# W_out products four steps behind W_in products instead of three, with a smaller space for GpSimd's DMA descriptors

## The chip, the core and the metric

The kernel runs on one core of a Trainium2 chip. The metric is device time in microseconds (us) of one execution; the time of a kernel is the median of its runs. The core has a matrix engine (TensorE, PE in the profile, with its weight loads as PEld), VectorE (DVE), ScalarE (ACT), GpSimd (POOL) and SyncE (SP), each with a queue of its own that is worked in order, and 16 DMA engines. Results of TensorE go to banks of PSUM, from which VectorE and ScalarE read.

## The reference

```python
def _attn_ref(x, w_r, w_i, b_r, b_i):          # x: 8 x 3008 x 256
    X = np.fft.rfft(x, axis=1)
    Xr, Xi = X.real.astype(np.float32), X.imag.astype(np.float32)
    Yr = Xr @ w_r - Xi @ w_i + b_r             # w_r, w_i: 256 x 256
    Yi = Xr @ w_i + Xi @ w_r + b_i
    Yr = np.sign(Yr) * np.maximum(np.abs(Yr) - 0.01, 0.0)
    Yi = np.sign(Yi) * np.maximum(np.abs(Yi) - 0.01, 0.0)
    y = np.fft.irfft(Yr.astype(np.float64) + 1j * Yi.astype(np.float64), n=x.shape[1], axis=1)
    return y.astype(np.float32)

def _moe_ref(x, w_in, w_out):                  # x: 24064 x 256, w_in: 256 x 2048
    h = x @ w_in
    g = h * np.cos(h)
    return (g @ w_out).astype(np.float32)      # w_out: 2048 x 256
```

The output of the first function, seen as 24064 tokens of 256 values, is the input of the second.

## The kernel before, in words

**Two halves that run interleaved.** For each of the 8 batches a Fourier half computes y (transforms as small matmuls, the products with w_r and w_i, the threshold, and the way back), and a second half, called MoE here, computes (h·cos h) @ w_out from it. While the MoE half of batch b runs, the Fourier work of batch b+1 is pulled in between its steps. `ahead` makes that work as a sequence of pieces with a planner's costs, and `pull` takes pieces as long as a budget, topped up at each step, allows it.

**MoE tiling.** Each batch has 6 token tiles (t) of 512 tokens (448 in the last), and each tile 16 chunks (f) of 128 hidden features. One (b, t, f) is a step; there are 768, and I number them through: step 16 is the first of tile t=1, step 96 the first of batch b=1, so step 227 is f=3 of t=2 in b=2.

**One step.** `moe_step` issues the W_in product of a step: every operand is split into a high part of TensorE's fp32r format and a rest, so it takes 6 matmuls into one PSUM bank `ph` (L923, L924, L925). From `ph` a chain of five instructions leads to g: ScalarE forms the integer k (L932), VectorE subtracts it (r, L933), ScalarE takes the sine (L935), VectorE multiplies by h (the product, L936, which sets `ph` free), and ScalarE casts to the high part `gh` (L938). The rest gl = u − gh follows on GpSimd for f%4 of 0 and 2 (L325) and on VectorE otherwise (L328). `u`, `gh` and `gl` are tiles in SBUF with a number of buffers each.

**W_out behind W_in.** The W_out product of a step, `second`, is not issued with its W_in product but SKEW steps later; a list `pend` holds the steps between. It takes 6 matmuls into two PSUM tiles `po` (L905, L906 with gh, L909 with gl), which add up over the 16 steps of a token tile. After the last one ScalarE copies both `po` to an SBUF tile `ob` (L913) and SyncE stores them. There is one buffer for each of the two `po` tiles, so the first W_out of a token tile waits for the copies of the tile before it.

**The Fourier work beside it** shares all engines: among it casts on ScalarE to `Xh` (L594, L602, L609), rests `Xl` on VectorE (through L328 as well), transposes on VectorE (L716, L717), matmuls such as L660 that use Xh and Xl, and loads of `xt` that GpSimd issues and then uses (L450). All matmul results except po go through a ring of 6 PSUM banks.

**What sets the order.** The code sets a program order, and the framework's scheduler puts each engine's instructions into the order that they have on the chip. A change in SKEW so moves instructions on every engine, not on PE alone.

Of the kernel before, what the change touches and what calls it, by code (L numbers as in the profile page):

```python
# [13 lines left out]
F32 = mybir.dt.float32  # L14
# [13 lines left out]
F64_HUGE = float(np.uint32((1150 << 20) | 0xFFE00).view(np.float32))  # L28
NFC = FF // 128
NTT = 6  # L30
SKEW = 3
XP_BUFS = 6
W_AT = (8, 16, 24, 32, 40, 48, 56, 64, 74)
W_ORDER = tuple(range(16))
# [142 lines left out]
def tile_body(ctx: ExitStack, tc, x, w_r, w_i, b_r, b_i, w_in, w_out,  # L177
              c_fq, c_sig, c_f3, c_ff, c_if, c_iw, c_sgn, out):
    nc = tc.nc
# [6 lines left out]
    pool = {}  # L186
# [145 lines left out]
    def fps(name):  # L332
        if len(ring) >= BANKS:
            assert ring[-BANKS][1]
        p = ps.tile([128, 512], F32, tag="f", name=name, bufs=BANKS)
        if "pro" not in pool:
            ring.append((p, []))
        return p
# [3 lines left out]
    def drained(p, ins):  # L342

        for q, readers in (side if "pro" in pool else ring)[-BANKS:]:
            if q is p:
                readers.append(ins.ins)
# [551 lines left out]
    def second(b, t, f, gh, gl):  # L898
        n = 512 if t < NTT - 1 else 448
        if f == 0:  # L900
            outs[0] = [ps.tile([128, 512], F32, tag=f"o{e}", name=f"po{e}", bufs=1) for e in range(2)]
        po = outs[0]
        for e in range(2):
            es = slice(128 * e, 128 * e + 128)
            mm(po[e][:, :n], wo[0][:, 0, f, es], gh[:, :n], start=f == 0, stop=False)  # L905
            mm(po[e][:, :n], wo[0][:, 1, f, es], gh[:, :n], start=False, stop=False)  # L906
        for e in range(2):
            es = slice(128 * e, 128 * e + 128)
            mm(po[e][:, :n], wo[0][:, 0, f, es], gl[:, :n], start=False, stop=f == NFC - 1)  # L909
        if f == NFC - 1:  # L910
            ob = stage_out("ob")
            for e in range(2):
                nc.scalar.copy(ob[:, 512 * e:512 * e + n], po[e][:, :n])  # L913
                nc.sync.dma_start(out[b, e, :, 512 * t:512 * t + n], ob[:, 512 * e:512 * e + n])

    def moe_step(b, t, f, pull):
        th, tl = xT[b, t]
        n = 512 if t < NTT - 1 else 448
        ph = fps("ph")
        h = ph[:, :n]  # L920
        fs = slice(128 * f, 128 * f + 128)
        for c in range(2):
            mm(h, win[:, 0, c, fs], th[:, c, :n], start=c == 0, stop=False)  # L923
            mm(h, win[:, 0, c, fs], tl[:, c, :n], start=False, stop=False)  # L924
            ins = mm(h, win[:, 1, c, fs], th[:, c, :n], start=False, stop=c == 1)  # L925
        if (b, t) == (0, 0) and f < 4:
            mark["ph"] = ins
        u = pool["mo"].tile([128, 512], F32, tag="u", name="u", bufs=4)
        k = u.bitcast(I32)
        gh = pool["mo"].tile([128, 512], F32R, tag="gh", name="gh", bufs=SKEW + 1)  # L930
        gl = pool["mo"].tile([128, 512], F32R, tag="gl", name="gl", bufs=SKEW + 1)
        nc.scalar.activation(k[:, :n], h, AF.Identity, bias=0.25, scale=1.0 / TWO_PI)  # L932
        nc.vector.scalar_tensor_tensor(out=u[:, :n], in0=h, scalar=1.0 / TWO_PI, in1=k[:, :n],  # L933
                                       op0=ALU.mult, op1=ALU.subtract)
        nc.scalar.activation(u[:, :n], u[:, :n], AF.Sin, bias=HALF_PI, scale=TWO_PI)  # L935
        product = nc.vector.tensor_tensor(out=u[:, :n], in0=h, in1=u[:, :n], op=ALU.mult)  # L936
        drained(ph, product)
        step = [nc.scalar.copy(gh[:, :n], u[:, :n])]  # L938
        step.append((rest_pool if f % 4 in POOL_GL else rest)(gl[:, :n], u[:, :n], gh[:, :n]))
        if f % 4 in POOL_GL:  # L940
            step.append(product)
        elif steps:
            step.append(steps[-1][1])
        steps.append(step)
        pend.append((b, t, f, gh, gl))
        pull()
        if len(pend) > SKEW:
            second(*pend.pop(0))
        pull()
# [93 lines left out]
    for b in range(NB):  # L1043
        fa = ahead(b)
        for t in range(NTT):
            budget = [0.0]
            open_ = [True]
            rate = (C_COST + share(b)) / (NFC - 1) / 2

            def pull():  # L1050
                budget[0] += rate
                while open_[0] and budget[0] > 0:
                    c = next(fa, None)
                    if c is None:
                        open_[0] = False
                    else:
                        budget[0] -= c

            for f in range(NFC):
                if (b, t) == (0, 0) and f in W_LATE:  # L1060
                    next(mw, None)
                moe_step(b, t, f, pull)
            while open_[0]:
                c = next(fa, None)
                if c is None:
                    open_[0] = False
            del xT[b, t]
# [27 lines left out]
```

## Time and profile before

| | |
|---|---|
| Runs | 2622.96, 2630.61 and 2635.15 us, median 2630.61 |
| Profiled execution | 2636.05 us, of which the span of the trace is 2634.3 |
| Granted clock of PE, mean | 0.992 |
| Busy share of the span | PE 98%, PEld 79%, VectorE 74%, ScalarE 62%, GpSimd 37% |
| Chain of work that ended last | PE 81%, VectorE 9%, ScalarE 3%, DMA 2% |

The busy share says how much of the span an engine worked; PE's matmuls overlap one another, so its share comes out a little high. The chain is followed back from the last instruction to whatever released each one. It lies mainly on PE; where it leaves PE, PE was waiting. The granted clock is the share of full speed that PE's clock was allowed in a stretch; full speed is 2.4 GHz, and the other level is 1.2 GHz.

### The profile page before, as it was taken

What the parts mean: (1) busy time and instruction counts of PE and PEld (TensorE: products, weight loads), DVE (VectorE), ACT (ScalarE), POOL (GpSimd) and SP (SyncE); (2) the same over time, 40 slices, a digit from 0 to 9 for tenths busy, and PEclk for the clock granted to TensorE, in tenths of its full rate; (3) what the DMA queues carried; (4) which work ended last, traced back from release to release, by engine and by line L of the source; (5) the groups of instructions that cost most, each with busy time, mean ns of one, the idle gap of its engine ahead of it and who ended that gap; (6) DMA issues with size and microseconds to landing.
All of it is one profiled execution on the core that took longest, in us unless ns stands there. A gap on an engine that the chain in (4) does not pass through costs nothing.

```text
span 2634.3 us, 42943 instructions
## 1 busy us (share of the span) xinstructions
PE 2571.2 (98%) x15961; PEld 2072.1 (79%) x15961; DVE 1943.9 (74%) x3089; ACT 1630.0 (62%) x3003; POOL 976.7 (37%) x946
## 2 busy tenths in 40 slices
PE   9899899999999999999999999999999999999999
PEld 7478678877788777887778877888778888888888
DVE  5688667877768777687776877778776777766665
ACT  5565556665666556656566565665666666666665
POOL 1124443444424443244433445334432333422222
PEclk9999999999999999999999999999999999999999
DMA  6534435354434443334442544326432343210000
GB/s 209 179 102 130 137 109 147 87 146 131 119 86 112 140 128 102 95 108 129 128 117 79 138 133 135 89 87 164 129 100 89 93 111 116 69 38 31 17 25 16
DMA packets 172953, 283.11 MB, mean 107 GB/s; under 512 B 15608, under 2 KB 114200, under 8 KB 169160
## 3 DMA queue, kind: packets, MB, share of 16 engines
q1 hardware_dynamic: 161896, 243.78, 32.9%
q0 software_dynamic: 10112, 35.53, 4.3%
q8 instruction: 126, 2.06, 0.3%
q10 hardware_dynamic: 736, 1.05, 0.1%
q14 instruction: 83, 0.68, 0.1%
HBM read 149.76 MB, written 130.55 MB: 106 GB/s over the span
## 4 chain that ended last, share of the span: by engine, by line
PE 81%; DVE 9%; ACT 3%; DMA 2%; issue 2%; POOL 1%; SPq 0%; DVEq 0%; ACTq 0%; POOLq 0%
PE ph L923 12%; PE po L905 11%; PE ph L924 11%; PE ph L925 11%; PE po L906 11%; PE po L909 11%; PE pw L660 2%; PE pw L661 2%; PE pw L662 2%; DVE u L936 2%; DVE u L933 2%; PE pc L377 1%; PE pb L377 1%; DVE Xl L328 1%; PE pw L656 1%
## 5 line engine op out<-in xcount | busy, mean ns | idle before, releaser
L325 POOL TENSOR_TENSOR gl<-u,gh 128x512 fp32r<-128x512 f32 (+1 forms) x384 | 501.4, 1306 | 1135.4 <-ACT gh L938 942.8
L935 ACT ACTIVATE u<-u 128x512 f32<-128x512 f32 (+1 forms) x768 | 478.1, 623 | 392.7 <-DVE u L933 391.8
L933 DVE SCALAR_TENSOR_TENSOR u<-ph,u 128x512 f32<-128x512 f32 (+1 forms) x768 | 513.6, 671 | 248.3 <-ACT u L932 247.2
L936 DVE TENSOR_TENSOR u<-ph,u 128x512 f32<-128x512 f32 (+1 forms) x768 | 518.0, 675 | 236.6 <-ACT u L935 225.4
L905 PE MATMUL po<-gh,wout 128*128 128x512 f32 (+1 forms) x1536 | 602.4, 392 | 28.0 <-ACT gh L938 28.0
L938 ACT CAST gh<-u 128x512 fp32r<-128x512 f32 (+1 forms) x768 | 467.8, 609 | 257.7 <-DVE u L936 254.6
L923 PE MATMUL ph<-xTh,win 128*128 128x512 f32 (+1 forms) x1536 | 605.2, 394 | 9.3 <-DVE u L936 7.6
L932 ACT ACTIVATE u<-ph 128x512 int32<-128x512 f32 (+1 forms) x768 | 447.7, 586 | 262.4 <-PE ph L925 255.9
L924 PE MATMUL ph<-xTl,win 128*128 128x512 f32 (+1 forms) x1536 | 597.2, 389 | 0.1
L925 PE MATMUL ph<-xTh,win 128*128 128x512 f32 (+1 forms) x1536 | 596.6, 388 | 0.0
L906 PE MATMUL po<-gh,wout 128*128 128x512 f32 (+1 forms) x1536 | 595.5, 388 | 0.0
L909 PE MATMUL po<-gl,wout 128*128 128x512 f32 (+1 forms) x1536 | 476.3, 388 | 0.3 <-POOL gl L325 0.2
L923 PEld LDWEIGHTS ph<-xTh,win 128*128 128x128 f32 x1536 | 290.0, 189 | 101.0 <-DVE u L936 22.5
L905 PEld LDWEIGHTS po<-gh,wout 128*128 128x128 f32 x1536 | 289.4, 188 | 100.6 <-ACT gh L938 38.5
L328 DVE TENSOR_TENSOR gl<-u,gh 128x512 fp32r<-128x512 f32 (+1 forms) x384 | 297.8, 776 | 79.6 <-ACT gh L938 73.5
L925 PEld LDWEIGHTS ph<-xTh,win 128*128 128x128 f32 x1536 | 290.2, 189 | 57.3
L909 PEld LDWEIGHTS po<-gl,wout 128*128 128x128 f32 x1536 | 287.2, 188 | 60.8 <-issue 4.9
L924 PEld LDWEIGHTS ph<-xTl,win 128*128 128x128 f32 x1536 | 290.3, 189 | 51.1 <-DVE xTl L891 0.6
L906 PEld LDWEIGHTS po<-gh,wout 128*128 128x128 f32 x1536 | 289.7, 189 | 50.9
L709 POOL TENSOR_TENSOR odd<-st 128x184 f32<-128x184 f32 (+1 forms) x112 | 67.4, 604 | 147.2 <-DVE st L686 117.0
L328 DVE TENSOR_TENSOR Xl<-z,Xh 128x384 fp32r<-128x384 f32 x112 | 110.3, 1013 | 12.0 <-ACT Xh L594 8.9
L660 PE MATMUL pw<-Xh,wf 128*128 128x384 f32 x336 | 115.5, 344 | 2.4 <-ACT Xh L609 2.2
(123 smaller groups left out, 2453.1 us busy)
## 6 DMA issues: line engine op xcount, KB each, us to landing
scrF<-at SPq DMA_DIRECT2D x28, 1024.0 KB
z<-scrF SPq DMA_DIRECT2D x112, 256.0 KB
scrT<-tr SPq DMA_DIRECT2D x56, 512.0 KB
y<-scrT SPq DMA_DIRECT2D x112, 256.0 KB
bt<-scr SPq DMA_DIRECT2D x94, 256.0 KB
scr<-ao SPq DMA_DIRECT2D x84, 256.0 KB
scr<-bo SPq DMA_DIRECT2D x224, 96.0 KB
out_dram<-ob SPq DMA_DIRECT2D x80, 256.0 KB
```

What stands on the lines that cost most here:

```text
L325: return nc.gpsimd.tensor_tensor(out=lo, in0=x, in1=hi.bitcast(F32), op=ALU.subtract)
L905: mm(po[e][:, :n], wo[0][:, 0, f, es], gh[:, :n], start=f == 0, stop=False)
L906: mm(po[e][:, :n], wo[0][:, 1, f, es], gh[:, :n], start=False, stop=False)
L909: mm(po[e][:, :n], wo[0][:, 0, f, es], gl[:, :n], start=False, stop=f == NFC - 1)
L923: mm(h, win[:, 0, c, fs], th[:, c, :n], start=c == 0, stop=False)
L924: mm(h, win[:, 0, c, fs], tl[:, c, :n], start=False, stop=False)
L925: ins = mm(h, win[:, 1, c, fs], th[:, c, :n], start=False, stop=c == 1)
L932: nc.scalar.activation(k[:, :n], h, AF.Identity, bias=0.25, scale=1.0 / TWO_PI)
L933: nc.vector.scalar_tensor_tensor(out=u[:, :n], in0=h, scalar=1.0 / TWO_PI, in1=k[:, :n], op0=ALU.mult, op1=ALU.subtract)
L935: nc.scalar.activation(u[:, :n], u[:, :n], AF.Sin, bias=HALF_PI, scale=TWO_PI)
L936: product = nc.vector.tensor_tensor(out=u[:, :n], in0=h, in1=u[:, :n], op=ALU.mult)
L938: step = [nc.scalar.copy(gh[:, :n], u[:, :n])]
```

## The change

SKEW becomes 4, so that a W_out product follows its W_in product by four steps. `gh` and `gl` have SKEW + 1 buffers and so get a fifth; `u` gets one too, by number. Each of the three is 2 KB in every partition. The room comes from the space that is set aside in SBUF for the descriptors of GpSimd's DMAs, 16384 bytes in each partition without the new argument and 8192 with it. The instructions and their number stay the same.

```diff
-SKEW = 3
+SKEW = 4
...
-        u = pool["mo"].tile([128, 512], F32, tag="u", name="u", bufs=4)
+        u = pool["mo"].tile([128, 512], F32, tag="u", name="u", bufs=5)
         k = u.bitcast(I32)
         gh = pool["mo"].tile([128, 512], F32R, tag="gh", name="gh", bufs=SKEW + 1)
         gl = pool["mo"].tile([128, 512], F32R, tag="gl", name="gl", bufs=SKEW + 1)
...
-    nc = _bacc.Bacc("TRN2", target_bir_lowering=False, num_devices=1)
+    nc = _bacc.Bacc("TRN2", target_bir_lowering=False, num_devices=1,
+                     dynamic_dma_scratch_size=8192)
```

How the order moves, at the places of which the prediction speaks.

ScalarE around the change from tile t=1 to t=2 in batch 2, from k(226) on, before. `u<-ph` is k, `u<-u` the sine, `gh<-u` the cast of a step; the two `ob<-po` are the copies that set the PSUM tiles of the old token tile free:

```order
L932 ACTIVATE u<-ph 128x512
L913 COPY ob<-po_8384 128x512
L913 COPY ob<-po_8385 128x512
L935 ACTIVATE u<-u 128x512
L932 ACTIVATE u<-ph 128x512
L938 CAST gh<-u 128x512
L594 CAST Xh<-z 128x2x8x24
L602 CAST Xh<-z 128x2x8x24 x2
L932 ACTIVATE u<-ph 128x512
```

The same place now:

```order
L932 ACTIVATE u<-ph 128x512
L935 ACTIVATE u<-u 128x512
L932 ACTIVATE u<-ph 128x512
L938 CAST gh<-u 128x512
L594 CAST Xh<-z 128x2x8x24
L602 CAST Xh<-z 128x2x8x24 x2
L913 COPY ob<-po_8421 128x512
L913 COPY ob<-po_8422 128x512
L935 ACTIVATE u<-u 128x512
```

The two copies stood right behind k(226) and now stand behind gh(226) and three casts of the Fourier work.

ScalarE around the change from t=2 to t=3 in batch 1, before; the first row is k(146), the first `gh<-u` is that of 146:

```order
L932 ACTIVATE u<-ph 128x512
L935 ACTIVATE u<-u 128x512
L913 COPY ob<-po_5754 128x512
L913 COPY ob<-po_5755 128x512
L938 CAST gh<-u 128x512
L594 CAST Xh<-z 128x2x8x24 x2
L932 ACTIVATE u<-ph 128x512 x2
```

The same place now:

```order
L932 ACTIVATE u<-ph 128x512
L935 ACTIVATE u<-u 128x512
L938 CAST gh<-u 128x512
L594 CAST Xh<-z 128x2x8x24
L932 ACTIVATE u<-ph 128x512
L594 CAST Xh<-z 128x2x8x24
L935 ACTIVATE u<-u 128x512
L932 ACTIVATE u<-ph 128x512
L913 COPY ob<-po_5775 128x512
L913 COPY ob<-po_5776 128x512
```

The copies stood ahead of gh(146) and now stand behind it, two casts, k(147), the sine of 147 and k(148).

## Rows read from the trace of the kernel before

**Rows 1.** Page, part 1: busy time, share of the span, instructions of each engine

```profile
PE 2571.2 (98%) x15961; PEld 2072.1 (79%) x15961; DVE 1943.9 (74%) x3089; ACT 1630.0 (62%) x3003; POOL 976.7 (37%) x946
```

**Rows 2.** Page, part 5, groups: busy us, mean ns | idle before, releaser

```profile
L933 DVE SCALAR_TENSOR_TENSOR u<-ph,u 128x512 f32<-128x512 f32 (+1 forms) x768 | 513.6, 671 | 248.3 <-ACT u L932 247.2
L938 ACT CAST gh<-u 128x512 fp32r<-128x512 f32 (+1 forms) x768 | 467.8, 609 | 257.7 <-DVE u L936 254.6
L932 ACT ACTIVATE u<-ph 128x512 int32<-128x512 f32 (+1 forms) x768 | 447.7, 586 | 262.4 <-PE ph L925 255.9
```

**Rows 3.** Waits, PE and PEld: us in total, times, longest us

```profile
PE po L905 <- ACT gh L938: 28.0, 15, 5.1
PE pc L367 <- DMA bt<-scr: 3.3, 1, 3.3
PEld po L905 <- ACT gh L938: 38.5, 25, 5.5
```

**Rows 4.** Timeline of PE, step f=3 of t=2: start, us, instruction [idle, releaser]

```profile
599.21 0.50 PE L905 MATMUL po<-gh,wout 128*128 128x512 f32 x1 [0.51 <-ACT gh L938]
...
917.45 0.50 PE L905 MATMUL po<-gh,wout 128*128 128x512 f32 x1 [1.85 <-ACT gh L938]
...
1235.37 0.52 PE L905 MATMUL po<-gh,wout 128*128 128x512 f32 x1 [2.10 <-ACT gh L938]
...
1553.66 0.50 PE L905 MATMUL po<-gh,wout 128*128 128x512 f32 x1 [0.63 <-ACT gh L938]
...
1871.03 0.50 PE L905 MATMUL po<-gh,wout 128*128 128x512 f32 x1 [1.85 <-ACT gh L938]
```

**Rows 5.** Timeline ahead of step 227 (b=2, t=2, f=3), 911 to 915 us

```profile
911.09 0.66 DVE L936 TENSOR_TENSOR u<-ph,u 128x512 f32<-128x512 f32 x1
...
911.36 0.39 PE L905 MATMUL po<-gh,wout 128*128 128x512 f32 x1
...
911.78 0.62 ACT L938 CAST gh<-u 128x512 fp32r<-128x512 f32 x1 [0.79 <-DVE u L936]
...
912.72 0.92 ACT L602 CAST Xh<-z 128x384 fp32r<-128x384 f32 x2
...
914.99 0.61 PE L909 MATMUL po<-gl,wout 128*128 128x512 f32 x2
```

**Rows 6.** Timeline around step 147 (b=1, t=3, f=3); last row: b=2

```profile
652.71 1.06 ACT L913 COPY ob<-po 128x512 f32<-128x512 f32 x2
...
653.33 0.50 PE L905 MATMUL po<-gh,wout 128*128 128x512 f32 x1
...
654.08 0.62 ACT L938 CAST gh<-u 128x512 fp32r<-128x512 f32 x1 [0.31 <-DVE u L936]
...
655.15 1.69 DVE L328 TENSOR_TENSOR Xl<-z,Xh 128x384 fp32r<-128x384 f32 x1 [0.64 <-ACT Xh L594]
...
660.32 0.50 PE L905 MATMUL po<-gh,wout 128*128 128x512 f32 x1 [1.92 <-ACT gh L938]
...
661.33 2.32 DVE L328 TENSOR_TENSOR Xl<-z,Xh 128x384 fp32r<-128x384 f32 x3
...
663.83 0.44 PE L660 MATMUL pw<-Xh,wf 128*128 128x384 f32 x1 [0.45 <-ACT Xh L609]
...
978.56 0.50 PE L905 MATMUL po<-gh,wout 128*128 128x512 f32 x1 [0.93 <-ACT gh L938]
```

**Rows 7.** Timeline of batch 0: GpSimd at its load, PE at step 43

```profile
273.15 1.29 POOL L450 TENSOR_TENSOR xe<-xt 128x512 f32<-128x512 f32 x1 [5.56 <-DMA xt<-in_dram]
...
294.74 0.79 PE L905 MATMUL po<-gh,wout 128*128 128x512 f32 x1 [4.87 <-ACT gh L938]
```

**Rows 8.** Windows: stretch, length, busy time and instructions by engine, PEclk, DMA, GB/s

```profile
104.00:116.00 12.00, 7.14 (x86) 4.09 (x78) 6.96 (x12) 5.55 (x11) 5.15 (x8) 0.72 0.58 139
655.00:665.00 10.00, 7.63 (x31) 5.15 (x31) 9.76 (x16) 7.77 (x17) 6.65 (x7) 1.00 0.40 121
915.00:925.00 10.00, 8.15 (x31) 6.56 (x30) 8.10 (x11) 5.15 (x11) 5.43 (x5) 0.83 0.48 104
```

## The prediction

> **What bounds the kernel now.** I read the engines' shares first: TensorE (PE) is busy 98% of the span, the next engine 74% [rows 1]. So only what PE waits for, and the clock that it is granted, can give or take time. The list of waits comes next [rows 3]: PE's first W_out matmul waits for gh, the cast at the end of a step's chain, in 15 places, 28.0 us in all. That is 1.1% of the span, and all that a longer lead of W_in over W_out can win at PE directly. It is also the only term that the change aims at, since the instructions stay the same.
>
> Going along PE's timeline, the 15 fall into three families. **A**: step f=3 of tile t=2 in batches b=1 to 5, waits 0.51, 1.85, 2.10, 0.63 and 1.85, together 6.9 [rows 4]. **B**: steps f=3 and 4 of tile t=3 in the same batches, four waits of 1.92 (one row stands for the four) and one of 0.93, together 8.6 [rows 6]. **C**: three in batch 0, the two long ones 4.87 [rows 7] and 5.1, the longest of all [rows 3]; the chain there stands behind a transpose that waits for GpSimd, which waits 5.56 us for a load of xt [rows 7]. With a few short ones that makes the 28.0.
>
> Beside the waits stands the clock. A batch-0 wait of 3.3 us on a DMA [rows 3] is followed by a stretch of 12 us whose granted clock is 0.72 [rows 8], a part of it at the lower of the two levels (1.2 against 2.4 GHz); that is 12 × 0.28 = 3.4 us lost behind 3.3 of waiting. After A's 1.85 at 917 the next 10 us show 0.83 (1.7 lost); after B's 1.92 at 660 they show 1.00 [rows 8]. So a wait near 2 us sometimes costs clock, a longer one does.
>
> **What the change does, part by part.** The descriptor space and the buffers add no instruction and are costed at nothing. What moves is the order. I take the places in turn, from the order of before and after, with times from the trace.
>
> *A.* PE runs W_out of step 224, the first of its tile, from 911.36, at 0.227 us a matmul (16 of them to 914.99), and reaches step 227 after 18, that is 4.1 us [rows 5]. There it waits, because the chain of 227 is late: gh of step 226 runs only at 911.78, since its product stood at 911.09 [rows 5]. In the new order the W_in of 227 stands six matmuls earlier on PE (1.37 us), while W_out of 227 is the same matmul number as before. If all of that reached the chain, gh(226) would start near 909.8 to 911.2. But ScalarE now has the two copies ob<-po, which empty the PSUM tiles of the old token tile, behind gh(226) and three casts; before, they stood ahead of it. The first W_out of the new tile needs the first of these copies. From gh(226)'s start: gh 0.52, two L602 0.83 (0.92 in their row, the ends overlapping), cast L594 0.42 as one of them, copy 0.6, in all 2.4, so the copy ends at 912.2 to 913.6. PE, with only 12 matmuls (2.74 us) between the last W_out of the old tile and the first of the new one instead of 18, is there at 911.1. **A wait of 1.1 to 2.5 us for the copy takes the place of the wait for gh.** Then 18 matmuls, and step 227 starts at 916.3 to 917.7 against 917.45: −0.45 in the middle (−1.15 to +0.25). Three large places −1.4, the two small ones −0.25 each (their gh wait is all there is to win): **−1.9** (−4.6 to +1.8). The clock behind the place I leave as it is, as a wait of about the same size stands 4 us earlier: 0 (−3.4 to +1.7).
>
> *B.* Already before, the first W_out of tile 3 starts when the copy ends: two copies from 652.71, 1.06 in all, so that the first is done half-way, and PE at 653.33 [rows 6]. There is no slack. In the new order, in b=1, 3 and 5, the copies stand behind gh(146), two L594 casts, the Sin of 147 and k(148). The Sin waits for VectorE's r(147), and that for the rest Xl (1.69 long in [rows 6]; I take 1.35) behind the first cast. Without copies ahead of it gh(146) starts at 652.2 to 653.0 (654.08 before). From there: 0.5 gh, 0.5 cast, 1.35 rest, 0.4 transpose, 0.6 r, 0.55 Sin, 0.5 k, 0.6 copy = 5.0, by [rows 2, 6] less the tenth that neighbours overlap. The copy ends at 657.2 to 658.0, where PE stands ready at 653.85: **a wait of 3.3 to 4.1 us**. Another 4.1 brings step 147 to 661.3 to 662.1 (660.32 before). Step 148 hangs on VectorE: gl(147), three rests (2.32, [rows 6]), r, product, then gh; W_out of 148 ends, and the Fourier matmul L660 starts, at 664.5 to 665.3 against 663.83: +0.7 to +1.5, three times, **+3.3**. In b=2 and 4 the copies stand behind gh(243) and two L602 casts and end near 657.9, and with 24 matmuls behind them the same point comes +0.1 to +0.9 late: twice, **+1.0**.
>
> *Clock at B.* Five waits of 3 to 4 us stand where waits of 1.92 and 0.93 stood, after which the clock was 1.00 [rows 8]. The nearest row is the wait of 3.3 with 3.4 lost behind it. The A rows say that some waits go without. I take half, 5 × 1.7 = **+8.5** (0 to +17), because the new waits begin just where the row of 3.3 lies and may fall short of it.
>
> *C.* W_in and W_out of steps 43 and 59 stand at the same matmul numbers in both orders, and what is late there is GpSimd's load: **0** (±2).
>
> *Rest.* The first tile change in batch 0 (step 16) gets its copies behind k(19) and 12 instead of 18 matmuls: **+1** (0 to 2.5). Short waits of the list's tail: **−1** (−2.5 to 0); a matmul starts every 0.227 us though it lasts 0.39, so up to 0.16 of each wait is already hidden.
>
> A rule weighed here. The trace has PE 98% busy, while the weight loads of the same instructions wait longer, 38.5 us in 25 places against 28.0 in 15 [rows 3]. The Trainium skill, page "Trainium Kernel Development and Optimization", paragraph "Reading a trace", says that matmul busy time is a bad measure of the distance to roofline since matmuls are pipelined. By that rule 10.5 us more could be won where waits go away; by the rows at most 0.16 in each of ten places, 1.6. I keep the rows.
>
> **Sum.** −1.9 + 3.3 + 1.0 + 8.5 + 0 + 1 − 1 = +10.9 us. The profiled execution took 2636.05, which gives 2646.9; on the median of the runs, 2630.61, it is **2641.5**. The ends of the terms that can go together give 2620 to 2661 for this case.
>
> **Rivals.**
> 1. *The waits go* (faster, chance 0.15). The copies come out early enough, because the casts ahead of them find their inputs ready, and the gh waits of A and B vanish: −6.9 − 8.6, the two large dips of A's clock −3.4, a share of what follows them −2.2: −21, 2609.5. For it: the lead in steps is a third longer, and gh(226) was late by less than one step. Against: the copies stand behind the casts in ScalarE's queue, and B had no slack before. Had the weight loads' 10.5 gone too, which I doubt, it would be 2599.
> 2. *One wait for another, no clock* (0.15). PE waits at the copies what it waited at gh, and the clock at B stays 1.00: +10.9 − 8.5 = +2.4 at most, with A's waits a little shorter 0: 2631. For it: 1.92 at 660 cost no clock. Against: the new wait is nearly twice as long.
> 3. *The clock falls each time* (slower, 0.11). The lower level follows at all five B, 3.4 each, 17; and A's chain gains nothing, since VectorE's transposes hold r(227), so A's wait of 1.1 to 2.5 adds 1.8 at five places, 9: with B's 4.3, −1 and +1 left out, about +30, less 2 for the short ones: 2659. It decides from the point where the copy ends over 3 us behind PE's arrival.
> 4. *The smaller descriptor space holds GpSimd's loads* (0.04). The loads of xt are issued from GpSimd in pairs; if the second of a pair had to wait for the first, each of 18 pairs could lose up to the 5.56 us wait of [rows 7]. GpSimd is busy 37%, which hides most; at the two places of C alone it is +8, at twelve of the pairs +67. The Trainium skill, page "DMA: Bandwidth & Descriptors", section "Terms", gives a descriptor as 16 bytes, which would leave room for 512 in 8192 bytes (an estimate from that page); no run here shows how many a load takes.
>
> **How the numbers follow.** Forecast 0.55, rivals 0.15, 0.15, 0.11, 0.04. A measurement of this kernel can tell about 0.5% from no change, that is under 2617.4 or over 2643.8. Faster: rival 1 nearly whole and the forecast's lower end, 0.17. Slower: rivals 3 and 4 (0.15) and of the forecast, centred 2 us below the bound, two fifths (0.22): 0.37. Same: 0.46. The range 2613 to 2661 cuts off most of rival 1 (0.12) and the top of rivals 3 and 4 (0.08).
>
> **What would show it.** In the trace after, PE's list of waits should show W_out waiting for ScalarE's ob copies, some 25 us in ten places, and A's waits for gh gone or under 1 us. At the five B the copies should end 3 to 4 us after PE is ready, and the granted clock of the 10 us behind should fall below 1.00 at some. C should stand as before, GpSimd's waits for xt too. If no wait for the copies shows, the order's place of them did not matter and the step on ScalarE's queue is wrong; if it shows and the clock stays, rival 2 is right.

## The result and the profile after

The changed kernel takes 2650.47 us (median of 6 runs, 2642.59 to 2653.23) against 2630.21 before (6 runs): a ratio of 1.0076, 95% interval 1.0061 to 1.0091. It is about 20 us slower. The forecast was 2641.5, in a range of 2613 to 2661: the direction is right, and so is the wait that it named, but the size was about half, and terms that missed in opposite directions kept it from being further off. The profiled execution has a span of 2650.6 us, 16.3 more than that of before.

The first view is the page's head after the change, with the busy time, share and instruction count of each engine; it answers to [rows 1].

```profile
span 2650.6 us, 42859 instructions
## 1 busy us (share of the span) xinstructions
PE 2573.2 (97%) x15961; PEld 2082.8 (79%) x15961; DVE 1940.7 (73%) x3089; ACT 1632.0 (62%) x3003; POOL 977.2 (37%) x946
```

PE is busy for the same time within 2 us, in a span that is 16 longer. So the time must be in what PE waits for. The list of PE's waits after the change (us in all, times, longest), which answers to [rows 3]:

```profile
PE po L905 <- ACT ob L913: 32.4, 11, 3.8
PE ph L923 <- DVE u L936: 10.1, 4, 6.5
PE po L905 <- ACT gh L938: 9.3, 3, 5.1
PE pi L367 <- DMA y<-scrT: 4.8, 3, 2.3
...
PEld po L905 <- ACT ob L913: 37.0, 11, 4.2
```

The wait for gh, 28.0 us in 15 places before, is down to 9.3 in 3, all in batch 0. On top stands a wait that the list of before does not have: the first W_out of a token tile waits for ScalarE's copy `ob<-po`, 32.4 us in 11 places. Ten of them are places A and B of batches 1 to 5; the eleventh is step 16, with 0.8.

The timeline of ScalarE and PE at B in batch 1 (start, us, instruction, [idle time before it, releaser]), which answers to [rows 6]:

```profile
652.30 0.50 ACT L594 CAST Xh<-z 128x384 fp32r<-128x384 f32 x1
654.59 0.63 ACT L935 ACTIVATE u<-u 128x512 f32<-128x512 f32 x1 [1.78 <-DVE u L933]
655.13 0.58 ACT L932 ACTIVATE u<-ph 128x512 int32<-128x512 f32 x1
655.60 1.06 ACT L913 COPY ob<-po 128x512 f32<-128x512 f32 x2
656.23 0.79 PE L905 MATMUL po<-gh,wout 128*128 128x512 f32 x1 [3.75 <-ACT ob L913]
```

ScalarE itself stands still for 1.78 us ahead of the sine, because VectorE's r comes late, and the two copies, whose data have long been ready, stand in the queue behind that sine and a k. PE has waited 3.75 us when the first copy is done. The matmul that then starts lasts 0.79 instead of 0.50 in [rows 6]: the clock has fallen.

At A in batch 2, the place of [rows 4, 5], it reads alike:

```profile
915.14 0.62 ACT L938 CAST gh<-u 128x512 fp32r<-128x512 f32 x1 [0.27 <-DVE u L936]
915.66 0.51 ACT L594 CAST Xh<-z 128x384 fp32r<-128x384 f32 x1
916.08 0.92 ACT L602 CAST Xh<-z 128x384 fp32r<-128x384 f32 x2
916.90 1.06 ACT L913 COPY ob<-po 128x512 f32<-128x512 f32 x2
917.53 0.50 PE L905 MATMUL po<-gh,wout 128*128 128x512 f32 x1 [3.06 <-ACT ob L913]
```

The order is the one shown ahead of the prediction, gh and three casts ahead of the copies, and ScalarE works through them without a pause.

For the clock, windows after the change, the first three around B in batch 1, the next behind A in batch 2, the last behind A in batch 3; the columns are the stretch, its length, busy time and instructions of PE, PEld, DVE, ACT and POOL, granted clock, DMA share and GB/s. They answer to [rows 8].

```profile
652.00:666.00 14.00, 10.25 (x40) 8.10 (x39) 11.98 (x17) 9.35 (x19) 7.97 (x7) 0.88 0.53 152
...
656.00:660.00 4.00, 3.77 (x10) 3.04 (x11) 3.34 (x6) 4.00 (x9) 0.90 (x1) 0.59 0.85 296
660.00:666.00 6.00, 6.00 (x28) 5.00 (x27) 4.64 (x6) 3.13 (x7) 3.66 (x4) 1.00 0.68 156
...
917.50:921.50 4.00, 3.97 (x12) 3.10 (x13) 4.00 (x7) 4.00 (x9) 3.14 (x3) 0.65 0.66 192
...
1240.00:1246.50 6.50, 6.12 (x15) 4.84 (x16) 6.50 (x9) 5.32 (x11) 4.06 (x3) 0.51 0.23 84
```

Behind the wait of 3.75 the granted clock is 0.59 over 4 us, so some 3.3 of them at 1.2 GHz, and 10 matmuls start there where some 17 would at 0.227 us. Behind the wait at A in batch 3 (3.46 us, 1240 us) the low level lasts 6.5 us. Over the whole run the mean granted clock fell from 0.992 to 0.986. The share that is missing, times the span, is 0.008 × 2634 = 21 us before and 0.014 × 2651 = 37 us after. A part of that lies inside the waits and costs nothing.

### The profile page after: what moved, and what is told of

The parts are those of the page before. It is cut to its first block, busy times and chain, and to the rows that moved or that the text cites. A ratio compares the mean times of both kernels' runs of the same rounds, so it can differ in the third digit from the quotient of the medians.

```text
span 2650.6 us, 42859 instructions
## 1 busy us (share of the span) xinstructions
PE 2573.2 (97%) x15961; PEld 2082.8 (79%) x15961; DVE 1940.7 (73%) x3089; ACT 1632.0 (62%) x3003; POOL 977.2 (37%) x946
## 4 chain that ended last, share of the span: by engine, by line
PE 78%; DVE 8%; DMA 5%; ACT 3%; issue 3%; POOL 3%; SPq 0%; DVEq 0%; ACTq 0%; POOLq 0%
PE po L905 11%; PE po L906 11%; PE po L909 11%; PE ph L923 11%; PE ph L924 10%; PE ph L925 10%; DMA xt<-in_dram 2%; PE pw L660 2%; PE pw L661 2%; PE pw L662 2%; DVE u L936 1%; DVE u L933 1%; PE pb L377 1%; PE pw L656 1%; DMA y<-scrT 1%
## 5 line engine op out<-in xcount | busy, mean ns | idle before, releaser
L325 POOL TENSOR_TENSOR gl<-u,gh 128x512 fp32r<-128x512 f32 (+1 forms) x384 | 494.7, 1288 | 1166.6 <-ACT gh L938 912.3
L905 PE MATMUL po<-gh,wout 128*128 128x512 f32 (+1 forms) x1536 | 605.8, 394 | 41.6 <-ACT ob L913 32.4
L909 PE MATMUL po<-gl,wout 128*128 128x512 f32 (+1 forms) x1536 | 486.4, 390 | 0.3 <-POOL gl L325 0.3
L905 PEld LDWEIGHTS po<-gh,wout 128*128 128x128 f32 x1536 | 293.0, 191 | 109.1 <-ACT ob L913 37.0
L906 PEld LDWEIGHTS po<-gh,wout 128*128 128x128 f32 x1536 | 293.5, 191 | 58.5 <-issue 5.7
L909 PEld LDWEIGHTS po<-gl,wout 128*128 128x128 f32 x1536 | 291.8, 190 | 56.1 <-POOL gl L325 0.7
```

Of the source, the lines that this page charges most:

```text
L325: return nc.gpsimd.tensor_tensor(out=lo, in0=x, in1=hi.bitcast(F32), op=ALU.subtract)
```

## The experiments

My theory was that the time went into PE's waits for the late copies and into the clock behind them. The rivals were the smaller descriptor space and the buffers; the longer lead itself (Fourier work and loads later); and that the copies' place does not matter. Ratios are to before, with their 95% interval.

**The change without its reordering.**

```diff
-        u = pool["mo"].tile([128, 512], F32, tag="u", name="u", bufs=4)
+        u = pool["mo"].tile([128, 512], F32, tag="u", name="u", bufs=5)
-        gh = ... bufs=SKEW + 1)
-        gl = ... bufs=SKEW + 1)
+        gh = ... bufs=SKEW + 2)
+        gl = ... bufs=SKEW + 2)
-    nc = _bacc.Bacc("TRN2", target_bir_lowering=False, num_devices=1)
+    nc = _bacc.Bacc("TRN2", target_bir_lowering=False, num_devices=1,
+                     dynamic_dma_scratch_size=8192)
```

> A lead of three steps as before, but with five buffers each for u, gh and gl and the descriptor space of 8192: the change without its reordering. PE's order is that of before but for one group of three matmuls. My theory (the time went into waits for the copies ob<-po and the clock behind them) gives 2630 us, within 4 us of before, no wait of W_out for a copy, and the waits for gh as before, 26 to 28 us. The rival that the smaller descriptor space or the buffers cost the time gives 2640 to 2650, with GpSimd's waits for xt longer than the 5.56 us of before.

Measured: 2629.07 us, ratio 0.9995 (0.9985 to 1.0004). PE's wait for gh is 24.5 us in 15 places; there is no wait of PE for a copy. Neither the space nor the buffers cost anything. All that the change does to the time comes from the order.

**The last W_out of a tile one step earlier, with a lead of four.**

```diff
         if len(pend) > SKEW:
             second(*pend.pop(0))
+        if pend[0][2] == NFC - 1:
+            second(*pend.pop(0))
```

> The changed kernel, but the W_out product of the last step of a token tile is issued one step earlier, three behind its W_in, right after that of the step before it. The copies stand in ScalarE's order where they stood before (ahead of gh(226), right behind the sine of 146) and 18 matmuls, not 12, lie between the old tile and the new one; the rest keeps a lead of four. My theory: PE's wait for the copies falls from 32 us to under 8, the low clock behind it goes, and with the waits for gh of the places A and B gone too the time is 2610 to 2628, below both kernels. The rival that the longer lead itself costs the time (Fourier work later, loads late, clock) gives 2643 to 2653, as the changed kernel.

Measured: 2603.75 us, ratio 0.9902 (0.9888 to 0.9917): 1% faster than before and some 46 us faster than the changed kernel. That is below the band that I gave. PE's and PEld's waits for gh, and the copies and the first W_out of the new tile at B in batch 1:

```profile
PE po L905 <- ACT gh L938: 13.4, 10, 5.1
...
PEld po L905 <- ACT gh L938: 20.0, 16, 5.6
```

```profile
644.25 0.63 ACT L935 ACTIVATE u<-u 128x512 f32<-128x512 f32 x1 [1.08 <-DVE u L933]
644.79 0.57 ACT L913 COPY ob<-po 128x512 f32<-128x512 f32 x1
...
646.77 0.58 ACT L913 COPY ob<-po 128x512 f32<-128x512 f32 x1
...
646.93 0.39 PE L905 MATMUL po<-gh,wout 128*128 128x512 f32 x1
```

The wait for copies is gone from the list, and of the waits for gh only two of batch 0 are longer than 0.8 us (5.1 and 4.0). The first copy is done at 645.4, and PE comes for it at 646.93 after 21 W_in matmuls without a pause. The mean granted clock is 0.993. A lead of four was worth having; what made it slow was the change of tile.

**W_out ahead of the first pull of Fourier work.**

```diff
         pend.append((b, t, f, gh, gl))
-        pull()
         if len(pend) > SKEW:
             second(*pend.pop(0))
         pull()
+        pull()
```

> The changed kernel with the W_out product of a step written ahead of the first pull of Fourier work in that step instead of behind it. In the order the copies now stand ahead of the casts L594 and L602 at place A in batches 1, 3 and 5, and at B some two ScalarE instructions earlier, still behind gh and the Fourier casts. My theory: PE waits for the copies some 15 to 24 us instead of 32, and the time is 2636 to 2646. If the place of the copies does not matter, it stays at 2650.

Measured: 2624.05 us, ratio 0.9979 (0.9967 to 0.9991), better than expected. The wait for copies is 6.7 us in 5 places, not 15 to 24: where the copies got ahead of the casts, and in B ahead of a sine and a k, most of the wait went at once; at A in batches 2 and 4, where they stayed behind the casts, 3.9 and 2.1 us are left. The profiled execution was the quickest of the ten, 2614.71 us, so the list belongs to a time 9 us under the median. The direction fits the theory; I had overrated how many instructions ahead of the copies must go.

**A lead of three, copies held behind gh.**

```diff
-                nc.scalar.copy(ob[:, 512 * e:512 * e + n], po[e][:, :n])
+                with tc.issue_after(steps[-1][0].ins):
+                    nc.scalar.copy(ob[:, 512 * e:512 * e + n], po[e][:, :n])
```

> A lead of three steps as before, buffers and space as before; only the two copies ob<-po of each token tile are held in ScalarE's queue behind the cast gh of the step that issues them. At B they come behind gh(146), at A behind gh(226), not behind the Fourier casts. My theory: at B, where there was no slack, PE now waits 1.5 to 2.5 us for a copy in five places, at A under 1 us, and some of these drop the clock: 2634 to 2645. If the place of the copies does not matter, 2630.

Measured: 2639.5 us, ratio 1.0052 (1.0034 to 1.0070), in the band, but not only for the reason given. The list (L-numbers are one higher here behind the edit):

```profile
PE po L905 <- ACT gh L939: 18.1, 13, 5.1
PE po L909 <- DVE gl L328: 10.0, 10, 1.5
...
PE po L905 <- ACT ob L914: 7.8, 7, 3.4
PE po L909 <- POOL gl L325: 4.9, 5, 1.5
```

At A the waits are under 1 us, as expected. At B the expectation failed: where I had set 1.5 to 2.5 us in five places, there is one wait of 0.5, and the longest, 3.4, is at step 16. The hold moved PE's order too: at B 24 matmuls lie between the two tiles instead of 21, so PE comes later (at 651.84 in batch 1, when the first copy had been done since 651.3). Twice as much stands at W_out waiting for gl, which was 0.2 us before, and the mean granted clock is 0.995, higher than before. That the time fell into the band is luck in part: the run agrees with the theory in its sign and does not test it at B.

**A lead of five.**

```diff
-SKEW = 4
+SKEW = 5
-        u = pool["mo"].tile([128, 512], F32, tag="u", name="u", bufs=5)
+        u = pool["mo"].tile([128, 512], F32, tag="u", name="u", bufs=6)
-                     dynamic_dma_scratch_size=8192)
+                     dynamic_dma_scratch_size=4096)
```

> A lead of five steps for every step, with six buffers each for u, gh and gl and a descriptor space of 4096. At most tile changes only 6 matmuls are left between the last W_out of the old tile and the first of the new one (18 in before, 12 in the changed kernel), and ScalarE's copies stand behind gh and k of steps further on. My theory: PE's wait for the copies grows from 32 us to 50 to 100, and the time to 2660 to 2700. The rival that more lead is bad only through late Fourier loads gives 2650 to 2660 with a wait for copies no longer than 32.

Measured: 2629.7 us, ratio 0.9998 (0.9987 to 1.0010). My expectation failed. There are more waits for copies, 16 instead of 11, but short ones, 21.0 us in all, the longest 2.8. At B in batch 1:

```profile
653.14 0.62 ACT L938 CAST gh<-u 128x512 fp32r<-128x512 f32 x1 [1.26 <-DVE u L936]
653.66 0.92 ACT L602 CAST Xh<-z 128x384 fp32r<-128x384 f32 x2
654.49 1.06 ACT L913 COPY ob<-po 128x512 f32<-128x512 f32 x2
655.12 0.19 PEld L905 LDWEIGHTS po<-gh,wout 128*128 128x128 f32 x1 [2.23 <-ACT ob L913]
655.12 0.50 PE L905 MATMUL po<-gh,wout 128*128 128x512 f32 x1 [1.81 <-ACT ob L913]
```

The copies start 1.2 us behind PE's arrival (654.49 against 653.31); with a lead of four it was 3.1 (655.60 against 652.48). In both kernels 3839 matmuls of PE stand ahead of this first W_out of the new tile: what moved is the last W_out of the old one, which has 12 matmuls behind it instead of 18, so that fewer matmuls between the tiles did not mean an earlier arrival. Counting matmuls between two instructions says how long PE needs from one to the other, not when it gets there.

**A lead of five, the last W_out at four.** The two edits above (lead five, and the last product early) together.

> A lead of five steps, but the W_out product of a tile's last step at a lead of four: six buffers, descriptor space 4096. By the order, the copies now stand where they stand in the changed kernel (behind gh(226) and three casts at A, 12 matmuls between the tiles). My theory: PE waits for the copies as in the changed kernel, 25 to 35 us, and the time is 2635 to 2655, although the lead is one longer than in the fast run with lead four. If the lead and not the copies' place gave that run its gain, this is at 2605 or below.

Measured: 2636.83 us, ratio 1.0024 (1.0014 to 1.0033); the wait for copies is 28.4 us in 11 places, the longest 4.1, as in the changed kernel. The band holds. It is also the plainest answer to the rival on the lead: with the copies in about the place that they have in the changed kernel the wait for them is back, at a lead of five as at four.

**A lead of three, the last W_out at two.** The edit of the run with lead four, on the kernel before.

> A lead of three steps as before, and the W_out product of a tile's last step at a lead of two; buffers and space as before. The copies stand one step earlier than before (ahead of k(226)). My theory: before has hardly a wait for the copies, so nothing is won there, the waits for gh stay (20 to 35 us, some of them at the last step of a tile, whose gh is now needed earlier): 2622 to 2640. If an earlier last product gives the gain by itself, whatever the lead, this is at 2605 to 2615.

Measured: 2634.75 us, ratio 1.0020 (1.0009 to 1.0031), in the band; the wait for gh stays at 27.1 us in 12 places. An early last product by itself gives nothing. Lead and tile change have to go together.

**Both helpful edits together.** The last product early, and W_out ahead of the first pull, with a lead of four.

> Lead four, the last W_out product of a tile one step earlier, and W_out written ahead of the first pull of Fourier work in each step: the two edits that each helped, together. The copies stand where they stood in the run with the first edit alone. My theory: no wait for copies is left to be won, so the time is within 5 us of that run, 2599 to 2609. If the second edit helps by another way (Fourier work later in the step), it is under 2599.

Measured: 2608.34 us, ratio 0.9914 (0.9900 to 0.9929), in the band. No wait for copies is left in either, and the second edit adds nothing.

**Only A, only B.**

```diff
+        if pend[0][1:3] == (1, NFC - 1) and 1 <= b <= 5:
+            second(*pend.pop(0))
```

For B the 1 is a 2.

> The changed kernel (lead four) with the last W_out product one step earlier only at the change from tile t=1 to t=2 in batches 1 to 5, place A. There the copies stand ahead of gh(226) and the casts again; at B they stand late as in the changed kernel. My theory: PE's wait for copies falls by the 14 us of A, the five B waits of 2.7 to 3.8 stay; the time is 2634 to 2644, against 2650 for the changed kernel. If A costs nothing, 2648 to 2652.

> The same, only at the change from t=2 to t=3 in batches 1 to 5, place B. My theory: the 18 us of copy waits at B go and with them the low clock behind B; the waits at A stay: 2622 to 2636. The gains of this run and of the one for A together are 35 to 50 us, as of both places at once. If B costs no more than A, 2634 to 2644.

Measured: A alone 2623.38 us, ratio 0.9980 (0.9970 to 0.9989); B alone 2627.79 us, 0.9997 (0.9987 to 1.0006). The waits for copies that are left, A's run first:

```profile
PE po L905 <- ACT ob L913: 14.7, 6, 3.7
```

```profile
PE po L905 <- ACT ob L913: 11.7, 5, 4.0
```

By the ratios times 2630, the changed kernel is 20.0 above before, the run with A mended 5.3 below, with B mended 0.8 below, and with all tile changes mended 25.8 below. So A takes back 25, B 21, together 46, and all of them 46. The two places add up, they carry the whole effect, and A is worth as much as B: there my expectation (A 6 to 16 us) failed. But A's 25 are not those of A's waits alone (13.9 us). With A mended the waits at B are still 1.3 to 3.7 us, and the clock falls behind only two of the five. A window behind the wait of 3.08 at B in batch 3 of that run:

```profile
1279.20:1291.20 12.00, 11.33 (x51) 9.32 (x52) 8.98 (x13) 8.26 (x17) 6.15 (x5) 1.00 0.63 172
```

**Filling the wait with work.**

```diff
-        for c in range(2):
+        for c in (0, 1, 0, 1) if f == 4 and t in (2, 3) and 1 <= b <= 5 else (0, 1):
             mm(h, win[:, 0, c, fs], th[:, c, :n], start=c == 0, stop=False)
```

In the second run the tuple is `(0, 1) * 3` at these steps.

> The changed kernel, with PE's wait for the copies filled with work: at A and B of batches 1 to 5 the six W_in matmuls of step f=4, which stand right ahead of the first W_out of the tile, are issued twice (the second pass writes the same values over the first). That is 60 matmuls, 13.7 us of PE work at 0.227 us each. My theory: this work lies inside the waits, which fall by about 1.4 us each; the time is 2640 to 2652, with fewer stretches at the low clock. If the waits are not where PE loses time, 2664.

> The same with the W_in matmuls of that step issued three times: 120 matmuls more, 27 us of PE work, at the ten places where PE waits about 3 us. My theory: the waits there fall to under 1 us and the clock stays at its upper level behind them; the work is paid by the waits, and what the clock gave away behind them, 5 to 12 us, comes back: 2638 to 2648. If the clock behind the waits costs nothing, 2648 to 2656; if the waits hide nothing, 2677.

Measured: with 60 matmuls more 2622.37 us, ratio 0.9974 (0.9965 to 0.9983); with 120 more 2634.42, 1.0018 (1.0007 to 1.0028). **With sixty superfluous matmuls the changed kernel is 27 us faster, with 120 it is 15 us faster.** A window over B in batch 1 and the wait for copies that is left, of the run with 60, then the same two of the run with 120:

```profile
649.00:663.00 14.00, 13.29 (x61) 10.90 (x60) 11.41 (x17) 9.55 (x19) 9.26 (x8) 1.00 0.54 152
```

```profile
PE po L905 <- ACT ob L913: 7.2, 6, 1.6
```

```profile
650.00:666.00 16.00, 16.00 (x75) 13.67 (x74) 12.31 (x19) 10.84 (x22) 9.16 (x8) 1.00 0.46 133
```

```profile
PE po L905 <- ACT ob L913: 0.4, 1, 0.4
```

The clock stays at 1.00 where it was 0.88 over a like stretch of the changed kernel. In the run with 120 the waits for copies fell by 32.0 us and 27.2 us of work (120 × 0.227) took their place, which leaves 5; PE's other waits grew by some 3 (that for y<-scrT from 4.8 to 6.4), which leaves 2; the time fell by 15. By the mean granted clock, 0.986 against 0.992, the clock gave back 0.006 × 2640 = 16 us, some of it inside the waits. So some 10 to 14 us of what the waits cost was the clock behind them. Neither run is quite clean, since the order moved a little beside the filling. At B in batches 1, 3 and 5 the copies stand behind the sine and gh of 147 and two L602 casts, not behind the sine of 147 and k(148). In the run with 60 the first copy stands ahead of gh and the casts again at A in batches 2 to 5, so that the waits fell by 25.2, more than the 13.7 of work: its 27 us are not the filling's alone. In the run with 120 that happened at A in batch 3 only, so it is the better test. Both times came out below the bands that I had given.

## Why the prediction was right, and where its sizes were off

To see each place's share in the change, I took the start of W_out of step f=8 in the tiles around it, in both traces, and the growth of the difference between them. With the longer lead PE has done six matmuls of W_in more at the mark in t=1 (84 lie between the marks in t=1 and t=2, 90 before) and as many at those in t=2 and 3; six are 1.4 us at 0.227, which I take off the difference at t=1. In batch 2, for t=1, 2 and 3, the starts are 880.19, 936.77 and 997.89 before and these after:

```profile
885.01 0.39 PE L905 MATMUL po<-gh,wout 128*128 128x512 f32 x1
...
941.00 0.40 PE L905 MATMUL po<-gh,wout 128*128 128x512 f32 x1
...
1006.33 0.39 PE L905 MATMUL po<-gh,wout 128*128 128x512 f32 x1
```

Differences of 4.8 less 1.4, that is 3.5, then 4.2 and 8.4: A gave +0.8, B +4.2. Over five batches, with the rest of the span:

| Term | Forecast | Measured |
|---|---|---|
| A, with its clock | −1.9 | +10.2 |
| B, with its clock | +12.8 | +10.8 |
| All up to A of batch 1 (C and step 16 in it; the short waits are counted here) | +1 − 1 | −5.5 |
| Between the tiles B and A, batches 1 to 5 | 0 | +3.0 |
| After batch 5 | 0 | −2.2 |
| Sum | +10.9 | +16.3 (profiled runs), +20 (medians) |

- **The new wait was right.** The prediction named the wait, the engine, its ten places, and their sum ("some 25 us in ten places"; 31.6 there). B was walked to 3.3 to 4.1 us; measured 2.75 to 3.75, at four of the five places 3.7. The claim that batch 0's C would stay holds for one of its two long waits (5.1 at step 43); the other, at step 59, shrank from 5.1 to 3.8. The stretch that holds C came out 5.5 shorter, outside the 2 us that I had allowed.
- **The step that failed is A**, both its wait and its clock. In the times of the trace before (3.46 taken off, the 4.82 at the mark in t=1 less 1.36) PE came for the copy at 911.0, as walked (911.1). But gh(226), which I had let start at 909.8 to 911.2, started at 915.14 − 3.46 = 911.7, no earlier than before (911.78): what W_in had gained on PE did not reach the end of the chain. (k(226), the first instruction behind W_in, started at 912.00 behind ScalarE's casts, with no pause ahead of it.) Over the five batches gh(226) and its fellows came from 1.4 us earlier to 2.2 later. From gh to the first W_out it took 2.4 us, as walked, so this W_out started at 914.1 and not at 912.2 to 913.6. The waits became 1.3 to 3.8 us (2.30, 3.06, 3.46, 3.75, 1.28), not 1.1 to 2.5: 13.9 in all where the waits for gh were 6.9.
- **The clock at A**, set to 0 "as a wait of about the same size stands 4 us earlier", fell behind four of the five waits, against two in before: some 8.5 us lost against 3.4. Rival 3 had A's outcome right, nothing gained in the chain and 9 us lost; its reason, transposes ahead of r(227) on VectorE, does not show in batch 2, where none stand between r(226) and r(227).
- **The clock at B was right in kind.** The half chance per place became a fall at all five, as rival 3 had it, but at 1.7 us lost in four of them and 3.4 in one, 10.2 in all, not 17. Waits (7.8 more) and clock together make 18.0, and the net of B is 10.8: about 1 of the difference is low clock inside the waits, the rest is time that PE lost there before in no listed wait (see the hidden waits below). That "a longer one does" cost clock does not hold as a rule: in the run with A mended the clock stayed at 1.00 behind 2.94 and 3.08.
- **Luck.** A missed by 12 us. That the whole missed by only 5 (profiled) to 9 (medians) is owed to the start of the run and its end, which came out 7.7 shorter for reasons that the prediction does not give.
- **The rest was not nothing.** A wait for the load y<-scrT grew from 2.3 to 4.8 us in all, the longest at 723 us in batch 1 with its own low clock behind it (0.79 over 8 us). Two of its three waits, 2.3 and 1.2, lie between the tiles B and A. Nothing in my working of the queues had moved SyncE's loads; how it came to be later I did not test.
- **The descriptor space was rightly costed at nothing**, by the first experiment: ratio 0.9995.
- **Hidden waits.** The trace showed 98% busy and waits of PE that were smaller than those of the weight loads. The rule of the Trainium skill, page "Trainium Kernel Development and Optimization", paragraph "Reading a trace", that busy time of matmuls misleads because they are pipelined, I had weighed as 10.5 us more to be won, and set aside for 1.6. In the run with lead four and an early last product PE's waits for gh fell by 14.6 us and the weight loads' by 18.5, only 3.9 more. But the matmuls' own starts say that the rule was nearer than the row. From 979.70 in the trace before, two L909 take 0.73 us from the first one's start to the start of the next matmul, where two times 0.227 would do, and no wait is listed. Summed over the W_in and W_out matmuls from 130 us on at the full clock, such time above 0.227 a matmul, less the listed waits, is 9.4 us before, 5.6 in the first experiment and 0.3 in this run, 0.4 in the changed kernel. That is 5 to 9 of the 10.5, where I had allowed 1.6.
- **Rival 1, the fast case, exists as a kernel.** Its number, 2609.5, was the time without the waits at A and B, 2599 with the weight loads' 10.5 as well; the run that frees the copies measured 2603.75, half-way between. What the rival lacked in the changed kernel is what it said must hold: that the copies come out early enough.

Open remain the later loads of y, what shortened the start of the run, why the clock falls behind some waits near 3 us and not behind others, and why the lead of five has shorter waits for copies at A than four; I looked at B alone.

## What to carry to other kernels

When a product is set further behind its source, look at the end of its accumulation first: an accumulator with one buffer makes the next tile wait for the copy that empties it, and a longer lead puts that copy later in its engine's queue. Pay the lead where the chain needs it and shorten it for the last product of a tile. And price a new wait on TensorE with the clock behind it: beside 32 us of waiting it cost some 10 to 14 more.

## What the runs showed of the hardware that I had not expected

Work without use can pay: 120 matmuls, 27.2 us of TensorE's time, put into waits of about 3 us, left the kernel 15 us faster, with a granted clock of 1.00 around B in batch 1, where 14 us had shown 0.88. With 60 it was 27 us faster, there in part because the order at A had moved as well. In the changed kernel nine of the ten waits for copies at A and B were followed by a stretch at the lower level (all but the shortest, 1.3 us), of which 4 us at 0.59 and 6.5 us at 0.51 are shown above. The length of a wait alone did not decide it: [rows 8] have 10 us at 1.00 behind a wait of 1.92 and 0.83 behind one of 1.85, and the run with A mended has 12 us at 1.00 behind one of 3.08.
